# Attention with a memory, then a gated feed-forward: all pacing waits taken out, the order of issue written anew

## The chip, the cores and the metric

The kernel runs on one core of one Trainium2 chip. The metric is the device time of one execution in microseconds (us), the median of three runs. Engines are named as in the profile: PE (TensorE, matmul; PEld its weight loads), DVE (VectorE), ACT (ScalarE), POOL (GpSimd) and SP (SyncE, which here only issues DMAs).

## What is computed

Cut to what matters; all tensors are float32 at the kernel's border, and the three weight matrices come as float64.

```python
B, H, S, D = 4, 8, 576, 64
scores = causal(q @ k.T / sqrt(D));  a = softmax(scores)
local = a @ v
q_p = where(q > 0, q, exp(q) - 1) + 1
mem_out = (q_p @ M_prev) / (q_p @ z_prev + 1e-6)
g = sigmoid(beta)
x = g * mem_out + (1 - g) * local          # to (B*S, H*D) = (2304, 512)
xn = x / sqrt(mean(x * x) + 1e-6) * rms_g
gate = xn @ w_gate;  val = xn @ w_val      # d_ff = 1536
out = (gate * sigmoid(gate) * val) @ w_out # (2304, 512)
```

## The kernel before

**Tiling.** The 2304 rows are 18 blocks of 128. Blocks 0 to 3 are the first 128 rows of each of the four batches (one key block each) and are computed in float32; the others work on pairs of float16 numbers (a high and a low part). Two blocks make a chunk of 256 rows for the feed-forward part, so there are nine chunks, and each runs over 12 column blocks F of the hidden width. Chunk 0 is in float32 too.

**The lead-in.** Until about 160 us the kernel loads and prepares what later stages use. The 24 weight tiles of w_gate and w_val (W0 to W23; eight for each third of the hidden width, four of the gate and four of the value) and the 12 of w_out arrive as float64. `f64_to_f32` makes float32 of a tile with two ACT ops (lines 1023 and 1027) and one DVE op (line 1033). Later `w_split` makes float16 pairs. The scales for these pairs come from Gram matrices, `gram` (line 293, matmuls called csum), of keys, values and weights; those of keys and values of batches 0 and 1 need all their blocks, so `all_stats` loads blocks ahead of their turn: kv_602 is block 4 (two loads, keys and values), kv_605 the tail block of batches 0 and 1, kv_818 block 5, and `load_pre` (line 998) brings those called pre.

**The first blocks.** For block 0 and 1: transposes (tp, line 548), scores (line 614), exponentials on ACT (line 680), probabilities times values (loc, line 831), memory (mem, line 804). POOL adds both parts (line 849). `x_norm` squares and sums on ACT (line 408) and makes the factor xs on POOL (lines 908 and 911): x0 is that of block 0, x1 of block 1. `x_float` makes a diagonal of it on DVE (line 922), multiplies on PE (xtp, line 925) and writes xT on DVE (line 926). Then the first projections `m_proj` (gv, line 1110 in float32, line 1117 in float16) can run, and behind them the transposes of block 2.

**What sets the order.** A table, ISSUE, holds for each of the five engines the whole sequence of its instructions as a text: a letter is a kind of step, a number a repetition, and ~n takes the n-th of those not yet issued. `issue_in_order` chains all instructions of an engine in this sequence. Each engine works through its queue in that order. SP's loads share eight completion semaphores with ACT's, so a load waits for the one eight places ahead of it.

**The pacing waits.** On top of the true dependencies, some instructions wait on an event that they do not need, by `after` and `paced`. Five kinds there are: the first csum matmul of each key or value block of batch 0 and 1 waits for x0 (batch 0) or x1 (batch 1) (GDE); the loads of blocks 4, 5, of the tail and those of `load_pre` wait for x1 (GDL); the two ACT ops of conversions 2 to 11 wait for the last sum of block 1, event e11 (CDP, CDE); the memset and the copies of the second batch pair's memory matrix on POOL wait for x1 (lines 776 and 789); and the load of w_out tile f waits for the begin of conversion 20 + f (PACE). These lines state them:

```python
GDE = ("x0", "x1")
GDL = ("x1", "x1")
PACE = 4
CDP = (2, 12)
CDE = "e11"
```

Of the kernel before, what the change touches and what calls it, by code (L numbers as in the profile page):

```python
# [31 lines left out]
GDE = ("x0", "x1")  # L32
GDL = ("x1", "x1")
# [13 lines left out]
XP = 4  # L47
XB = 0
HLB = 5
RING = 5  # L50
PACE = 4
EARLY = 8
HTAG = ("v16", "v16", "v16", "v16")
CDP = (2, 12)
CDE = "e11"
# [12 lines left out]
GP = -600  # L68
# [1478 lines left out]
```

## Time and profile before

| | us |
|---|---|
| median of 3 runs | 604.43 |
| lowest and highest run | 602.52, 607.53 |
| the profiled execution, its own time | 602.39 |
| its span, first to last instruction | 600.5 |
| PE busy in it | 579.4 (96%) |
| DVE busy | 427.4 (71%) |
| ACT busy | 395.6 (66%) |
| POOL busy | 130.5 (22%) |

Times in the rows below are counted from the begin of the span; 1.9 us of the execution lie outside it. A row of the timeline gives the start, the time until the last end of a merged group, the engine, the line, the operation, what is written and read, the count, and in brackets the idle time of the engine before it with what ended it.

### The profile page before, as it was taken

To read this page: it belongs to the slowest core of one execution; us is meant where nothing else is said; L and a number is where in the kernel's file an instruction comes from. 1 tells how busy PE (TensorE), PEld (TensorE's weight loads), DVE (VectorE), ACT (ScalarE), POOL (GpSimd) and SP (SyncE) were. 2 spreads that over 40 slices of the span, in tenths; PEclk is the share of its full clock that TensorE was granted. 3 is DMA by queue.
4 is the path that set the end of the run, shared out by engine and by line. 5 is a ranking of instruction groups with operands and counts; after the bars stand their busy time and mean duration, and the time that the engine had idled before them with its cause. 6 is when DMAs were issued, how large, how long until landed. Compare 5 with 4: busy or idle time off the path is not lost.

```text
span 600.5 us, 15733 instructions
## 1 busy us (share of the span) xinstructions
PE 579.4 (96%) x6082; PEld 454.3 (76%) x6082; DVE 427.4 (71%) x1278; ACT 395.6 (66%) x856; POOL 130.5 (22%) x219
## 2 busy tenths in 40 slices
PE   6899999999899999999999999999999998999996
PEld 5778887678677778777777777777878776777774
DVE  3777998999998767776866777987885666642221
ACT  5889697998887667576657677876774454533221
POOL 2310012033332222131202221222122212121211
PEclk9899999999999999999999999999999999999999
DMA  7999555678879877977495789578884375441001
GB/s 249 365 319 395 152 172 157 154 155 160 189 138 182 136 137 164 147 149 147 85 186 125 135 157 170 117 140 142 137 166 80 70 115 97 86 67 28 10 1 53
DMA packets 183788, 87.57 MB, mean 146 GB/s; under 512 B 165793, under 2 KB 165793, under 8 KB 183713
## 3 DMA queue, kind: packets, MB, share of 16 engines
q1 hardware_dynamic: 180640, 81.82, 63.8%
q10 hardware_dynamic: 3072, 4.74, 2.4%
q8 instruction: 48, 0.79, 0.6%
q14 instruction: 28, 0.22, 0.1%
HBM read 37.77 MB, written 4.72 MB: 71 GB/s over the span
## 4 chain that ended last, share of the span: by engine, by line
PE 69%; DMA 15%; DVE 7%; ACT 6%; issue 2%; SPq 1%; POOL 0%; ACTq 0%; DVEq 0%; POOLq 0%
PE gv L1117 31%; PE out L1191 6%; PE out L1192 6%; PE out L1193 6%; DMA PT<-P 5%; PE gv L1110 4%; PE sc L625 4%; PE csum L293 2%; DMA kv<-in_qkv_dram 2%; DMA wgv<-in_moe_w_val_dram 2%; ACT junk L408 1%; PE sc L648 1%; PE loc L763 1%; DMA wgv<-in_moe_w_gate_dram 1%; PE loc L745 1%
## 5 line engine op out<-in xcount | busy, mean ns | idle before, releaser
L1117 PE MATMUL gv<-xT,wgv 128*128 128x256 f16 x2304 | 328.5, 273 | 2.0 <-DVE th L1138 2.0
L1117 PEld LDWEIGHTS <-wgv 128*128 128x128 f16 x2304 | 213.9, 98 | 47.2 <-issue 1.7
L1156 POOL TENSOR_TENSOR h<-th,h 128x256 f16<-128x256 f32 x88 | 64.8, 739 | 251.2 <-ACT h L1155 225.5
L688 ACT ACTIVATE S<-S,nm 128x256 f32<-128x256 f32 (+3 forms) x112 | 70.5, 639 | 39.9 <-DVE nm L631 19.7
L625 PE MATMUL sc<-kT,qT 128*128 128x128 f16 x576 | 85.2, 219 | 0.8 <-DVE nm L631 0.4
L1135 DVE SCALAR_TENSOR_TENSOR th<-th,gv 128x256 f32<-128x256 f32 x96 | 40.0, 416 | 63.0 <-ACT th L1134 61.6
L707 DVE SCALAR_TENSOR_TENSOR P<-S,P 128x512 f16<-128x512 f32 (+2 forms) x96 | 66.7, 695 | 24.1 <-ACT P L202 23.9
L1134 ACT ACTIVATE th<-gv,wt 128x256 f32<-128x256 f32 x96 | 44.9, 467 | 56.8 <-PE gv L1117 53.4
L202 ACT ACTIVATE P<-S 128x512 f16<-128x512 f32 (+2 forms) x96 | 57.8, 605 | 12.8 <-DMA PT<-P 11.7
L1191 PE MATMUL out<-wo,h 128*128 128x512 f16 x176 | 65.7, 379 | 0.2 <-ACT res L1168 0.2
L1192 PE MATMUL out<-wo,h 128*128 128x512 f16 x176 | 65.6, 379 | 0.0
L1193 PE MATMUL out<-wo,h 128*128 128x512 f16 x176 | 65.6, 379 | 0.1
L631 DVE CUSTOM_DVE_ANT_0 S<-sc,mask,qsc 128x256 f32<-128x256 f32 (+2 forms) x96 | 57.8, 610 | 10.6 <-PE sc L625 10.0
L1155 ACT CAST h<-th 128x256 f16<-128x256 f32 x88 | 34.8, 398 | 36.5 <-DVE th L1138 34.4
L625 PEld LDWEIGHTS <-qT 128*128 128x128 f16 x576 | 50.6, 98 | 9.9 <-issue 1.0
L745 PE MATMUL loc<-v,PT 128*128 128x65 f16 x288 | 46.0, 193 | 3.4 <-DMA PT<-P 2.4
L1138 DVE SCALAR_TENSOR_TENSOR th<-th,wt,gv 128x256 f32<-128x256 f32 x96 | 45.6, 476 | 1.3
L1110 PE MATMUL gv<-xT,wgv 128*128 128x256 f32 x192 | 46.5, 384 | 0.0
L747 PE MATMUL loc<-v,PT 128*128 128x65 f16 x288 | 46.2, 193 | 0.0
L746 PE MATMUL loc<-v,PT 128*128 128x64 f16 x288 | 45.3, 193 | 0.0
L1110 PEld LDWEIGHTS gv<-xT,wgv 128*128 128x128 f32 x192 | 34.9, 192 | 7.1 <-issue 1.9
L896 POOL TENSOR_TENSOR t<-t,t 128x256 f32<-128x256 f32 x28 | 21.3, 764 | 64.2 <-DVE t L893 60.1
(226 smaller groups left out, 980.0 us busy)
## 6 DMA issues: line engine op xcount, KB each, us to landing
kv<-in_qkv_dram SPq DMA_DIRECT2D x40, 256.0 KB, 3.8
q<-in_qkv_dram SPq DMA_DIRECT2D x18, 256.0 KB, 3.9
wo<-in_moe_w_out_dram SPq DMA_DIRECT2D x8, 512.0 KB, 4.6
out_dram<-res ACTq DMA_DIRECT2D x16, 256.0 KB, 2.4
wo<-in_moe_w_gate_dram SPq DMA_DIRECT2D x7, 512.0 KB, 7.9
wgv<-in_moe_w_val_dram SPq DMA_DIRECT2D x7, 512.0 KB, 8.7
qT<-qT SPq DMA_DIRECT2D x28, 128.0 KB, 3.0
wgv<-in_moe_w_gate_dram SPq DMA_DIRECT2D x5, 512.0 KB, 7.9
```

The costliest lines, as they stand in the source:

```text
L202: got = fn(*p, **k)
L625: nc.tensor.matmul(t[:, g * w + j * P : g * w + (j + 1) * P], qT[n][:, t2, h, :], kT[blk_of[(b, j)]][:, h, :], start=(t2 == 0), stop=(t2 = ...
L631: nc.vector.tensor_tensor_reduce(out=s[:, g * w : (g + 1) * w], in0=t[:, g * w : (g + 1) * w], in1=mask[:, m0 : m0 + w], scale=qsc[n][:, 5 ...
L688: nc.scalar.activation(v_, v_, AF.Exp, bias=nm[:, g : g + 1], scale=-1.0)
L707: m = nc.vector.scalar_tensor_tensor(out=p16[:, w : 2 * w], in0=s[:, :w], scalar=PSCALE, in1=p16[:, :w], op0=ALU.mult, op1=ALU.subtract)
L745: nc.tensor.matmul(a, phi_, vhi, start=(j == 0), stop=False)
L1110: nc.tensor.matmul(o, wgv[:, 1 + p, o0 : o0 + P], xT[0][:, cc, at], start=(cc == 0), stop=(cc == NC - 1))
L1117: nc.tensor.matmul(o, lhs, xT[c][:, rhs, :], start=(cnt == 0), stop=(cnt == 3 * NC - 1))
L1156: nc.gpsimd.tensor_tensor(h16[:, 1], th, h16[:, 0], ALU.subtract)
L1191: nc.tensor.matmul(o, hh, whi, start=(f == 0), stop=False)
L1192: nc.tensor.matmul(o, hh, wlo, start=False, stop=False)
L1193: nc.tensor.matmul(o, hl, whi, start=False, stop=(f == NF - 1))
```

## The change

All five kinds of pacing wait are taken out, with what served them (`after`, `paced`, the events, the priority around `gram`). No operation is added or removed and no buffer changes. The table ISSUE is written anew for all five engines; it holds the same instructions. The core of the diff, with a line or two of the table:

```diff
-GDE = ("x0", "x1")
-GDL = ("x1", "x1")
...
-PACE = 4
...
-CDP = (2, 12)
-CDE = "e11"
...
 ISSUE = {
     "PE": (
-        "T3T~1T~1T3Z2T12SS~1S~2S~3S3T4S2S~1S~2S~3T4uS4hu3h2ThT4u~2Tu2T2h4uT4h8ss~3ss~2ss~1s~1R3R~1R~1R~1R~1RsZG3G~5G~5G~5"
...
+        "T8Z2T12SS~1S~2SS~2S2T4uS2S~1S~2S~3T4S4uhu2h2sT2hT4u~2TuTuh4uT4h4s~3s~3h4s~3s~3ss~6sR3R~1R~1R~1R~1Rss~4s~4s~4G2G~"
...
-            m = nc.tensor.matmul(acc[:, :P], w, w, start=first and g == 0, stop=last and g == 3)
-            if g == 0 and ev:
-                after(m, event[ev])
+            nc.tensor.matmul(acc[:, :P], w, w, start=first and g == 0, stop=last and g == 3)
...
-            ins = nc.sync.dma_start(out=stage[n][:, j], in_=qkv[at_row[n], :, j, :])
-            if ev:
-                after(ins, event[ev])
+            nc.sync.dma_start(out=stage[n][:, j], in_=qkv[at_row[n], :, j, :])
...
-                with tc.high_priority(GP):
-                    gram(csum["kv", b, j], src[j][r], i == 0, i == NI, GDE[b])
+                gram(csum["kv", b, j], src[j][r], i == 0, i == NI)
...
-        m = nc.gpsimd.memset(mb, 0.0)
-        if pr:
-            after(m, event['x1'])
+        nc.gpsimd.memset(mb, 0.0)
...
-            m = nc.gpsimd.tensor_copy(pairs[b // 2][r, b % 2, :, t * D : t * D + D], m4[r, :, t, :])
-            if b > 1:
-                after(m, event['x1'])
+            nc.gpsimd.tensor_copy(pairs[b // 2][r, b % 2, :, t * D : t * D + D], m4[r, :, t, :])
...
-        if p - PACE in begun:
-            tc.add_manual_dep(
...
-            ins = nc.sync.dma_start(out=t, in_=qkv[at_row[blk_of[(b, i)]], :, j, :])
-            if GDL[b]:
-                after(ins, event[GDL[b]])
+            nc.sync.dma_start(out=t, in_=qkv[at_row[blk_of[(b, i)]], :, j, :])
...
-        begun[p] = nc.scalar.activation(dst, r[:, :, 1], AF.Prelu, scale=2.0 ** -112, alpha=2.0 ** 32)
-        late = CDP[0] <= p < CDP[1]
-        if late:
-            after(begun[p], event[CDE])
-        m = nc.scalar.activation(
+        nc.scalar.activation(dst, r[:, :, 1], AF.Prelu, scale=2.0 ** -112, alpha=2.0 ** 32)
+        nc.scalar.activation(
...
-        if late:
-            after(m, event[CDE])
```

What the table sets is shown at three places. The line numbers of the changed kernel are its own: 293 is again csum, 815 is loc, 908 xtp, 833 the sum on POOL, 891 and 894 the two ops of xs, 951 a weight load, 357 a kv load.

PE, before, at the end of the first two blocks' attention (loc_370 is that of block 1, kv_96 holds block 0, csum_608 and csum_613 gather keys and values):

```order
L548 MATMUL tp<-ident,S 128x128 x4
L831 MATMUL loc_370<-kv_101,PT_293 128x64 x4
L831 MATMUL loc_370<-kv_101,PT_341 128x64 x4
L293 LDWEIGHTS kv_96
L293 MATMUL csum_608<-kv_96 128x128
```

Six further csum follow there, and then xtp. PE of the change, at the same place:

```order
L543 MATMUL tp<-ident,S 128x128 x4
L815 MATMUL loc_370<-kv_101,PT_293 128x64 x4
L293 LDWEIGHTS kv_96
L293 MATMUL csum_613<-kv_96 128x128
L293 LDWEIGHTS kv_96
L293 MATMUL csum_613<-kv_96 128x128
L815 MATMUL loc_370<-kv_101,PT_341 128x64 x4
```

Two csum now stand between the loc matmuls; one more stands some rows ahead of these, five behind them, and then xtp. One of the five, and three between xtp and gv, read a half of kv_602, which before was read behind the first 32 gv only.

POOL, before, around the two factors xs (t_0 and t_1 are the sums of block 0 and 1):

```order
L849 TENSOR_TENSOR t_0_315<-t_0_315,t_0_338 128x4x64 x2
L908 TENSOR_SCALAR xs<-xs 128x1
L849 TENSOR_TENSOR t_1_328<-t_1_328,t_1_377 128x4x64 x2
L911 TENSOR_TENSOR xs<-xs,few 128x1
L908 TENSOR_SCALAR xs<-xs 128x1
L911 TENSOR_TENSOR xs<-xs,few 128x1
```

POOL of the change, the same instructions:

```order
L833 TENSOR_TENSOR t_0_315<-t_0_315,t_0_338 128x4x64 x2
L891 TENSOR_SCALAR xs<-xs 128x1
L894 TENSOR_TENSOR xs<-xs,few 128x1
L833 TENSOR_TENSOR t_1_328<-t_1_328,t_1_377 128x4x64 x2
L891 TENSOR_SCALAR xs<-xs 128x1
L894 TENSOR_TENSOR xs<-xs,few 128x1
```

The second op of x0 now stands ahead of block 1's two sums instead of behind them.

SP, before, from the second load of block 0 on (a gate tile that goes to wo is one of the second third, one that goes to wgv here is one of the first):

```order
L359 DMA kv_96<-in_qkv_dram 128x512
L985 DMA wo<-in_moe_w_gate_dram 128x512 x2
L985 DMA wgv<-in_moe_w_gate_dram 128x512
L372 DMA wo<-in_M_prev_dram 64x512
L985 DMA wgv<-in_moe_w_gate_dram 128x512
L403 DMA q_192<-in_qkv_dram 128x512
L985 DMA wgv<-in_moe_w_val_dram 128x512
L985 DMA wo<-in_moe_w_gate_dram 128x512
L985 DMA wgv<-in_moe_w_gate_dram 128x512
L387 DMA kv_2_0_194<-in_qkv_dram 128x512
```

SP of the change, from the same load on:

```order
L357 DMA kv_96<-in_qkv_dram 128x512
L368 DMA wo<-in_M_prev_dram 64x512
L399 DMA q_192<-in_qkv_dram 128x512
L357 DMA kv_101<-in_qkv_dram 128x512
L951 DMA wo<-in_moe_w_gate_dram 128x512
L383 DMA kv_2_0_194<-in_qkv_dram 128x512
L357 DMA kv_602<-in_qkv_dram 128x512
L951 DMA wgv<-in_moe_w_val_dram 128x512 x2
L951 DMA wgv<-in_moe_w_gate_dram 128x512
```

Two of the three gate tiles of the second third have moved behind the first eight tiles (one of them by 26 places, one by 11), and a half of kv_602 has come from place 30 of the queue to place 14. Further down, W15 moves from place 39 to 46, and the last halves of the pre loads of batch 1 by 4 to 9 places back. Over the whole table an instruction of DVE, ACT, POOL or SP stands on average one to five places from where it stood, one of PE two to eleven out of 5857.

## Rows read from the trace of the kernel before

**Rows 1.** Busy us by stretch: length, PE, PEld, DVE, ACT, POOL (x instructions), PE clock, DMA share, GB/s

```profile
22.70:26.20 3.50, 1.10 (x8) 0.97 (x8) 1.68 (x7) 0.93 (x3) 2.16 (x4) 0.93 1.00 397
26.20:32.56 6.36, 5.98 (x27) 5.26 (x28) 3.69 (x9) 5.74 (x13) 1.76 (x4) 0.50 1.03 348
32.56:39.40 6.84, 6.84 (x35) 5.94 (x34) 4.46 (x9) 5.64 (x11) 1.31 (x5) 1.00 1.02 282
39.40:43.30 3.90, 2.76 (x29) 2.25 (x26) 3.73 (x15) 2.74 (x6) 0.79 (x2) 1.00 1.01 331
43.30:105.00 61.70, 61.70 (x439) 51.36 (x438) 51.57 (x194) 50.98 (x118) 6.03 (x14) 1.00 0.65 222
105.00:165.00 60.00, 58.01 (x504) 43.32 (x504) 59.42 (x164) 54.73 (x120) 16.89 (x21) 1.00 0.78 164
165.00:585.00 420.00, 415.51 (x4869) 323.47 (x4867) 286.27 (x802) 256.73 (x534) 93.78 (x150) 1.00 0.65 118
```

**Rows 2.** Who waited for whom, 0 to 60 us: total us, times, longest us

```profile
ACT junk L408 <- POOL t L849: 2.6, 1, 2.6
...
PE csum L293 <- POOL xs L911: 1.8, 1, 1.8
...
PE csum L293 <- DMA pre<-in_qkv_dram: 1.0, 1, 1.0
```

**Rows 3.** PE in order of time, 23 to 42 us

```profile
23.26 1.10 PE L831 MATMUL loc<-kv,PT 128*128 128x64 f32 x8 [0.57 <-DVE t L847]
26.21 0.93 PE L293 MATMUL csum<-kv 128*128 128x128 bf16 x7 [1.84 <-POOL xs L911]
26.94 4.08 PE L925 MATMUL xtp<-diag,t 128*128 128x128 f32 x16
...
32.03 7.39 PE L1110 MATMUL gv<-xT,wgv 128*128 128x256 f32 x32
...
41.28 0.23 PE L293 MATMUL csum<-pre 128*128 128x128 bf16 x1 [1.01 <-DMA pre<-in_qkv_dram]
41.38 0.63 PE L548 MATMUL tp<-ident,kv 128*128 128x128 f32 x4
```

**Rows 4.** What SP's queue waited for, 26 to 60 us

```profile
SPq L359 <- POOL stt L413: 0.3, 1, 0.3
```

**Rows 5.** DVE in order of time, 24 to 32 us

```profile
24.41 0.42 DVE L847 TENSOR_TENSOR t<-loc,den 128x256 f32<-128x256 f32 x1 [0.38 <-PE loc L831]
26.19 0.29 DVE L922 TENSOR_SCALAR diag<-ident,xs 128x128 f32<-128x128 f32 x1 [1.36 <-POOL xs L911]
27.34 1.07 DVE L922 TENSOR_SCALAR diag<-ident,xs 128x128 f32<-128x128 f32 x1 [0.86 <-POOL xs L911]
...
30.63 1.29 DVE L926 TENSOR_TENSOR xT<-xtp,few 128x512 f32<-128x512 f32 x2 [1.81 <-PE xtp L925]
```

**Rows 6.** POOL in order of time, 23 to 27 us

```profile
23.18 0.19 POOL L908 TENSOR_SCALAR xs<-xs 128x1 f32<-128x1 f32 x1 [0.84 <-ACT junk L408]
24.03 0.72 POOL L849 TENSOR_TENSOR t<-t,t 128x256 f32<-128x256 f32 x1 [0.66 <-DVE den L842]
...
25.59 0.57 POOL L911 TENSOR_TENSOR xs<-xs,few 128x1 f32<-128x1 f32 x1
```

**Rows 7.** DMA issues, 0 to 60 us: count, KB each, median us to landing

```profile
kv<-in_qkv_dram SPq DMA_DIRECT2D x14, 256.0 KB, 8.3
...
wgv<-in_moe_w_val_dram SPq DMA_DIRECT2D x7, 512.0 KB, 8.7
...
pre<-in_qkv_dram SPq DMA_DIRECT2D x8, 256.0 KB, 5.8
...
M<-in_M_prev_dram SPq DMA_DIRECT2D x4, 128.0 KB, 7.9
```

**Rows 8.** ACT in order of time, at two places

```profile
25.66 0.63 ACT L408 ACTIVATE junk<-t 128x512 bf16<-128x512 f32 x1 [2.57 <-POOL t L849]
...
55.29 0.68 ACT L1023 ACTIVATE wgv<-wgv 128x512 f32<-128x512 f32 x1
```

**Rows 9.** SP's queue in order of time, at 43 us

```profile
43.52 0.66 SPq L359 DMA_DIRECT2D kv<-in_qkv_dram  x1
```

**Rows 10.** The weight loads of line 985, 0 to 70 us

```profile
DMA to landing us min/median/max: 3.5/7.8/11.2
```

More of the change, by code (lines that the diff above doesn't have):

```diff
@@ new lines @@
+        "6G~6G~6GG~5G2G~3G6Zs2Zs2Ts2T3s~2s~2T4sT2s2T2S8sG5s~4G3u2G2sGu2G5T4s~3ss~2ss~1ss~4s~4s3s~1s~1sT4G6g5g~11Zg5T4g5g~"
+        "1g~1g~1g~1g~1g~1g~1g~1g~1g~1Zg~1g~1g~1g~1g~1GgGh3G2ZG2TGZG2sGss~2s~2hT2s2s~2s~2Tss~1ss~1s~1s~1s2s~4s2s~2ss~1ss~1"
+        "s~1s~1s~1Ts~5s~5s~5s~5sTsGT2G3gG4g4h3sgs2hg2s4g14ZgZg2SS~1S~2S~3g~7g~7g~7g~7g~7g~7g~7g~7g2g~5g~5g~5g~5g~5gg~4S4g"
+        "TuGg5G3TG3gGu~1u~1T2Z2g9ug5DgD~1h4Z2DTGT3G4DGDGDGh3GhG6D~1DG~1G~1G~1G3DG3D6G4DG2G~2GG~1G~1G~1DG~1G20D~1SGD~2DGS~"
+        "7G8S~7G3DS~7GS~7S~7S~7G2S4S~3S3G2G~6G3M~8M~8MM~7GM~7M~7MM~6M~6SMGM4G3MG6SGS6G2SG2DMG3S3G3S4G3SGD2G15SG19S7ZG4PG7"
@@ L147 @@
+        "3kFl~1blrl~1l~1rkrL2FlL2blrLr~1rkL3l~1lFlL2XrL2bXr~1rkbL2lFL2rL2lr~1LXrkL2rL2Flr~1L3lLbXkrLlLlLFL3rLbLm~1XrL2l2r"
+        "mkL2FL4rXLrblklrL2kFL3bLl2L2rkl2r2FXbrLXLr~1rLklLlm2L2FL4bL3XrL2r~1krkLbFrr~1rkL2XFL3bLrL2XrkLrL2FLrL2rkLXLrLFL1"
+        "1X2"
     ),
@@ L285, in total, with gram @@
         return t[:, :n]
-    def gram(acc, src, first, last, ev=""):
+    def gram(acc, src, first, last):
         hi = src.bitcast(BF16).rearrange("p (f w) -> p f w", w=2)[:, :, 1]
@@ L354, in load_kv @@
     @keep("l")
-    def load_kv(n, ev=""):
+    def load_kv(n):
         tag = "kvt" if is_tail[n] else "kv"
@@ L716, in attn_memory_moe_kernel @@
     accs = {}
-    def after(ins, ev):
-        tc.add_manual_dep(
-            ins.ins, ev.ins.name,
-            mybir.DependencyInfo(mybir.DependencyClass.Sync, mybir.DependencyReason.SCHED_ONLY),
-            reason="pace",
-        )
     @keep("P")
@@ L848, in evac32 @@
         part = t1s[n][:, four(n, g4), :]
-        event["e%d%d" % (n, g4)] = nc.gpsimd.tensor_tensor(part, part, t2, ALU.add)
+        nc.gpsimd.tensor_tensor(part, part, t2, ALU.add)
     @keep("M")
@@ L950, in attn_memory_moe_kernel @@
     NR = RING
-    begun = {}
-    def paced(ins, p):
-        if p in (2 * NC + XP, 2 * NC + XP + 1) and XB in xdone:
-            tc.add_manual_dep(
-                ins.ins, xdone[XB].ins.name,
-                mybir.DependencyInfo(mybir.DependencyClass.Sync, mybir.DependencyReason.SCHED_ONLY),
-                reason="pace",
-            )
-        if p - PACE in begun:
-            tc.add_manual_dep(
-                ins.ins, begun[p - PACE].ins.name,
-                mybir.DependencyInfo(mybir.DependencyClass.Sync, mybir.DependencyReason.SCHED_ONLY),
-                reason="pace",
-            )
     def hold(p, at):
@@ L1011, in load_wo @@
         raws["o", f] = r
-        ins = nc.sync.dma_start(out=r.bitcast(I64), in_=w_out[f * P : (f + 1) * P, :])
-        paced(ins, len(pcs) + f)
-    event = {}
+        nc.sync.dma_start(out=r.bitcast(I64), in_=w_out[f * P : (f + 1) * P, :])
     @keep("U")
@@ L1277, in all_stats @@
         stat_begin(b)
-        load_kv(NA + b, GDL[b])
+        load_kv(NA + b)
         if b == 0:
-            load_kv(tails[0], GDL[b])
+            load_kv(tails[0])
         for i in range(NI + 1):
```

140 lines of the change are left out of this document (68 added, 72 removed).

## Prediction

> **What bounds the kernel now.** I read the busy time by stretches first [rows 1]. TensorE (PE) is the engine to watch: from 43.3 us to 105 us it is busy in 61.7 of 61.7 us, and from 165 us to 585 us in 415.5 of 420. What can still be won lies ahead of 43 us, and a little between 105 and 165 us, where PE misses 2.0 us and VectorE (DVE) is busy for 59.4 of 60 us. All five kinds of pacing wait stand in the first 110 us, so I looked there for what they cost. [...]
>
> Then I asked who waits for whom in the first 60 us [rows 2]. Two PE waits there touch the change. The statistics matmuls (csum, line 293) waited 1.8 us, once, for xs of line 911: this is a pacing wait (x0) itself. And a csum waited 1.0 us for a load called pre. PE in order of time shows what stands around them [rows 3]: eight loc matmuls at 23.26, an idle 1.84 us, seven csum at 26.21, the sixteen records of the first normed block pair (xtp) at 26.94, the first projections (gv, 32 records, 7.39 us) at 32.03, and the csum on pre at 41.28, behind which block 2's transposes stand in the same queue.
>
> **The change part by part.** *The waits themselves.* Of all that are taken out, the trace shows an engine stopping at two: the csum wait of 1.84 us, and 0.3 us on SP's queue, where a kv load (line 359) waits behind GpSimd (POOL) line 413, the op after x1 [rows 4]. The paced conversions on ScalarE (ACT) and the paced copies on POOL show no wait of their own: ACT idles 2.57 us ahead of the second square sum (line 408), but for POOL's line 849, its true input [rows 2]. So the waits alone are worth at most 1.84 + 0.3 = 2.1 us, and less where an engine behind them had nothing to do anyway: xtp needs the diagonal of line 922, which ran at 26.19 for 0.29 us [rows 5], so without the csum wait xtp would have begun at about 26.5 instead of 26.94, 0.4 us.
>
> *Statistics ahead of the lull (PE order).* The new order puts csum matmuls of block 0 between the loc matmuls, from 20 us on. They cost the same and fill time in which PE idles. By count, the 3.50 us before 26.2 us then hold 1.10 us, eight csum (seven took 0.93 us at the low clock, about half at the high one), and the first six xtp records (below), about 2.5 us in all.
>
> *Block 0's norm ahead of block 1's sum (POOL order).* Now line 911 for x0 stands behind both sums of block 1: line 908 is done at 23.37, and line 911 runs at 25.59 [rows 6]. In the new order 911 follows 908 at once, so x0 is there near 23.9. The sum that it is put ahead of began at 24.03, so it is not delayed. The diagonal then runs on DVE near 24.8, after the last line 847, and xtp's first six records (block 0) are done before block 1's diagonal, which keeps its 27.34 [rows 5]. Ten records are left. Sixteen took 4.08 us [rows 3], so ten take 2.55 us at the low clock, and about half at the high one: from 27.7 to 30.2 or 29.0 instead of 31.02. xT (two DVE ops, 1.29 us) and gv follow 0.8 to 2.0 us earlier, so gv begins between 30.0 and 31.2.
>
> *The clock.* Ahead of the low stretch PE did 1.10 us of work in 3.50 us [rows 1]; in the new order it is busier there, about 2.5 us, so I take it that the clock holds. The bounds are a low stretch as now, and one that is later and covers gv. [...]
>
> *Loads (SP order).* All are 256 KB (kv, pre) or 512 KB (weights), M 128 KB [rows 7]. In the new order one half of kv_602 comes forward by 16 places, ahead of seven of the first eight weight tiles (W0 to W7), and two gate tiles of the second third go behind them. Up to the last of the eight I count 8.4 MB before and 7.6 MB now, at 0.35 to 0.40 MB per us [rows 1] 2.0 to 2.3 us sooner. The conversions on ACT are then less held up too: behind the second square sum, which keeps its 25.66 [rows 8], 12 ops of about 0.57 us each stand until the eight tiles are converted, where there were 15: 1.7 us sooner. So weights do not hold gv, which ends 6.8 us (7.39 less the slow start) after it begins: between 36.9 and 38.7, depending on the clock.
>
> *The next wait.* Behind gv the first matmul that needs a late load is no longer csum on pre (11.25 MB into the queue, waited for until 41.28) but csum on the other half of kv_602, 10.5 MB in. 0.75 MB at 0.28 to 0.33 MB per us [rows 1] is 2.3 to 2.7 us, so it lands at about 38.8. That is later than gv's end at either clock. PE waits there, and block 2's transposes follow at 39.4 instead of 41.4: 2.0 us sooner. This load sets the gain, not the clock.
>
> *From there on.* From 43.3 to 105 us PE has no idle time, so what it starts sooner it ends sooner. DVE must follow, since it is the bound between 105 and 165 us; it is busy for 51.6 of 61.7 us before that, so it has 10.1 us of cover. If that cover were gone the 2.0 us would be lost. Everything behind is the same work in nearly the same order: instructions stand a few places from where they stood. I book 0, with 2 us to either side, the size of PE's loss in 105 to 165 us.
>
> The sum: the profiled execution took 602.39 us; less 2.0 is 600.4. The median of the three runs is 2.0 above that execution (604.43), so I predict 602.4.
>
> **The rivals.** *The order alone did the pacing.* In-order queues hold their order without any wait, so nothing but noise changes: 604.4. For it speaks that only 2.1 us of pacing waits can be seen; against it, that the csum wait stood on the way to gv.
>
> *The clock falls later, over gv.* If the low stretch begins at 28 and lasts 6.4 us as now [rows 1], gv begins at 31.2 and is slow until 34.4; in those 3.2 us it does 1.6 us of work, so it ends near 39.6 instead of waiting from 38.0 for the load that lands at 38.8. The gain is 0.8 less, 1.2: 603.2. It decides only from the point where gv ends behind 38.8.
>
> *Slower: a weight tile comes late.* With the pacing gone, loads that nobody needs yet stand ahead of needed ones: the last value tile of the second third (W15) moves from 12.5 MB into the queue to 15.25 MB. At 15.0 MB stands kv_818 now, and it is issued at 43.52 [rows 9]; so W15 would be issued near 44 and, with the 8.7 us of its kind [rows 7], land at 52.7. ACT converts it at 55.29 now [rows 8], at 53.3 if all runs 2.0 us ahead: 0.6 us of slack. With the 11.2 us of the slowest weight load [rows 10] it lands at 55.2, 1.9 us late, and as ACT's queue is in order, the scores, copies and conversions behind it stop too and the gain is gone. From there each further us goes onto the end; with W13, W14 and the pre loads of the second pair, which stand by it, late by 3 us in all it is 607.4. Against it: most of these loads have slack of some us. [...]
>
> *DVE turns out as the bound.* If the new order leaves DVE idle for half of its 10.1 us of cover more before 105 us, the saturated stretch behind it starts late: +5 and no gain, 609.4. Nothing in the profile asks for it, but nothing there is hidden either.
>
> **How the numbers follow.** A gain of 1 to 4 us as summed 0.48; the order alone 0.22; the clock 0.09; the late tile 0.11; DVE, or a like loss behind 165 us, 0.10. The predicted time is that of the first. The range takes in the second to fourth and most of the fifth at the top, and at the bottom 2.0 us for the open term and 2 us for the spread of runs (602.5 to 607.5): 598.0 to 609.4. Over 1% (about 6 us, what a measurement of this kernel can tell from no change) faster needs both of these at once and a clock that holds: 0.08. Over 1% slower is the last case and a part of the late tile: 0.12. Within 1%: 0.80.
>
> **What would show it.** Right: no csum wait on xs; xtp in two parts, the first near 25 us; gv from about 30 to 31 us; PE waiting for kv_602 near 38 us; block 2's transposes near 39.4; PE full until 105. The load term is wrong if PE waits past 40 us for kv_602, the clock term if the granted clock is 0.50 behind 33 us, the last term if PE's idle time behind 105 us differs by more than 2 us, and the whole if ACT waits for a weight load between 50 and 60 us.

## The result and the profile after

Six runs of each kernel on the same chip gave a median of 603.47 us before (601.17 to 607.53) and 597.01 us after (596.68 to 599.18). The ratio is 0.9892, with a 95% interval of 0.9848 to 0.9935. The forecast was 602.4 us (598.0 to 609.4): the direction was right, the gain was three times what was forecast, and it fell outside the range.

The two profiled executions are no typical pair. That of before (602.39 us) lies 1.1 us below its median; that of after (599.18 us, span 597.2) is the slowest of its six. So they show 3.2 of the 6.5 us between the medians. More sets of runs came with the experiments, and one plain fact about them is needed for every number below: the 97 runs of the kernel before fall into two groups with nothing between, 58 from 599.4 to 604.6 us (median 601.7) and 39 from 606.3 to 611.6 us (median 608.2). Over all 97 the median is 602.6. The changed kernel's 18 runs lie from 593.2 to 599.9 us, median 596.7, with no gap.

The busy time by stretches of the profile after, as [rows 1] of before (length, then busy us of PE, its weight loads, DVE, ACT and POOL, the granted clock, the DMA share, GB/s):

```profile
22.70:26.20 3.50, 2.41 (x21) 1.96 (x19) 1.89 (x7) 3.13 (x8) 2.22 (x4) 1.00 1.02 315
26.20:32.56 6.36, 3.55 (x18) 2.99 (x19) 4.40 (x9) 6.36 (x14) 2.59 (x7) 0.76 1.03 309
32.56:39.40 6.84, 6.84 (x25) 5.67 (x24) 3.04 (x7) 3.54 (x7) 1.58 (x4) 0.73 0.97 307
39.40:43.30 3.90, 3.90 (x34) 3.42 (x32) 2.74 (x12) 2.98 (x7) 0.00 (x0) 1.00 1.03 370
43.30:105.00 61.70, 61.70 (x438) 51.34 (x437) 53.73 (x201) 52.30 (x120) 5.75 (x11) 1.00 0.63 220
105.00:165.00 60.00, 58.43 (x515) 43.44 (x514) 54.54 (x163) 53.60 (x119) 15.68 (x23) 1.00 0.80 160
165.00:585.00 420.00, 417.77 (x4890) 325.65 (x4888) 286.98 (x802) 259.59 (x536) 93.20 (x152) 1.00 0.65 119
```

PE in order of time after, as [rows 3] (start, us until the last end of the group, operation, count, and in brackets the idle time ahead of it and what ended it; for the wait of 2.48 us the row names a conversion on DVE's line 989, but what these matmuls read is block 1's diagonal, and it ended at 28.34 us):

```profile
23.25 1.10 PE L815 MATMUL loc<-kv,PT 128*128 128x64 f32 x8 [0.47 <-DVE t L831]
...
25.07 0.94 PE L908 MATMUL xtp<-diag,t 128*128 128x128 f32 x6 [0.42 <-DVE diag L905]
28.48 1.56 PE L908 MATMUL xtp<-diag,t 128*128 128x128 f32 x10 [2.48 <-DVE wgv L989]
...
31.00 9.78 PE L1066 MATMUL gv<-xT,wgv 128*128 128x256 f32 x32 [0.52 <-DVE cb L460]
...
41.34 0.28 PE L543 MATMUL tp<-ident,kv 128*128 128x128 f32 x1
```

The csum wait of 1.84 us is gone, xtp comes in two parts, gv begins 1.0 us sooner. But the granted clock, which was low ahead of gv in [rows 1], is now low over gv (0.76 and 0.73 of full in the second and third stretch), so gv takes 9.78 us instead of 7.39, and block 2's transposes stand at 41.34 us, where they stood at 41.38 in [rows 3]. **In this execution the lead gained nothing.** The gain is further back: PE's idle time from 105 to 585 us is 3.80 us (1.57 and 2.23) against 6.48 us (1.99 and 4.49) in [rows 1].

Who waited for whom on PE from 105 to 585 us (us in total, times, longest us). Before:

```profile
PE loc L745 <- DMA PT<-P: 2.4, 4, 1.6
PE gv L1117 <- DVE th L1138: 2.0, 2, 1.7
PE loc L745 <- DVE t L874: 0.9, 1, 0.9
```

After:

```profile
PE loc L733 <- DMA PT<-P: 1.9, 3, 1.6
```

The three longest waits of before in this stretch, PE in order of time:

```profile
159.25 0.27 PE L1117 MATMUL gv<-xT,wgv 128*128 128x256 f16 x1 [1.66 <-DVE th L1138]
...
474.19 0.19 PE L745 MATMUL loc<-v,PT 128*128 128x65 f16 x1 [0.85 <-DVE t L874]
...
502.64 0.20 PE L745 MATMUL loc<-v,PT 128*128 128x65 f16 x1 [1.62 <-DMA PT<-P]
```

None of the three is left after. A new wait of 1.57 us stands there at 146.36 us, for transposed probabilities.

### The profile page after: what moved, and what is told of

It reads as the page before. It is cut to its first block, busy times and chain, and to the rows that moved or that the text cites. A ratio compares the mean times of both kernels' runs of the same rounds, so it can differ in the third digit from the quotient of the medians.

```text
span 597.2 us, 15713 instructions
## 1 busy us (share of the span) xinstructions
PE 577.9 (97%) x6082; PEld 453.3 (76%) x6082; DVE 422.9 (71%) x1278; ACT 397.3 (67%) x856; POOL 127.6 (21%) x219
## 4 chain that ended last, share of the span: by engine, by line
PE 87%; DMA 8%; ACT 1%; SPq 1%; DVE 1%; issue 1%; POOL 0%; ACTq 0%; DVEq 0%; POOLq 0%
PE gv L1073 38%; PE gv L1066 8%; PE out L1149 7%; PE out L1147 7%; PE out L1148 7%; PE sc L620 5%; PE out L1139 3%; DMA PT<-P 3%; DMA wgv<-in_moe_w_val_dram 3%; PE csum L293 2%; PE sc L643 1%; PE loc L751 1%; PE loc L733 1%; PE loc L734 1%; PE loc L735 1%; PE mem L849 1%
## 5 line engine op out<-in xcount | busy, mean ns | idle before, releaser
L1073 PE MATMUL gv<-xT,wgv 128*128 128x256 f16 x2304 | 342.4, 273 | 0.0
L1073 PEld LDWEIGHTS <-wgv 128*128 128x128 f16 x2304 | 210.8, 98 | 50.6 <-issue 2.8
L1112 POOL TENSOR_TENSOR h<-th,h 128x256 f16<-128x256 f32 x88 | 62.9, 719 | 255.0 <-ACT h L1111 229.7
L620 PE MATMUL sc<-kT,qT 128*128 128x128 f16 x576 | 90.9, 219 | 0.0
L702 DVE SCALAR_TENSOR_TENSOR P<-S,P 128x512 f16<-128x512 f32 (+2 forms) x96 | 65.3, 683 | 18.8 <-ACT P L202 18.4
L733 PE MATMUL loc<-v,PT 128*128 128x65 f16 x288 | 49.4, 193 | 1.9 <-DMA PT<-P 1.9
L1066 PE MATMUL gv<-xT,wgv 128*128 128x256 f32 x192 | 49.6, 400 | 0.5 <-DVE cb L460 0.5
L735 PE MATMUL loc<-v,PT 128*128 128x65 f16 x288 | 49.8, 193 | 0.0
L734 PE MATMUL loc<-v,PT 128*128 128x64 f16 x288 | 48.9, 193 | 0.0
L1066 PEld LDWEIGHTS gv<-xT,wgv 128*128 128x128 f32 x192 | 36.2, 200 | 9.7 <-issue 4.0
```

The source lines that it names most:

```text
L620: nc.tensor.matmul(t[:, g * w + j * P : g * w + (j + 1) * P], qT[n][:, t2, h, :], kT[blk_of[(b, j)]][:, h, :], start=(t2 == 0), stop=(t2 = ...
L702: m = nc.vector.scalar_tensor_tensor(out=p16[:, w : 2 * w], in0=s[:, :w], scalar=PSCALE, in1=p16[:, :w], op0=ALU.mult, op1=ALU.subtract)
L735: nc.tensor.matmul(a, plo, vhi, start=False, stop=(j == nb - 1))
L1066: nc.tensor.matmul(o, wgv[:, 1 + p, o0 : o0 + P], xT[0][:, cc, at], start=(cc == 0), stop=(cc == NC - 1))
L1073: nc.tensor.matmul(o, lhs, xT[c][:, rhs, :], start=(cnt == 0), stop=(cnt == 3 * NC - 1))
L1112: nc.gpsimd.tensor_tensor(h16[:, 1], th, h16[:, 0], ALU.subtract)
```

## The experiments

The theories after the result: **A**, the gain comes from the order behind the lead (from about 105 us on), where PE's stalls went; **B**, it comes from the waits taken out and the lead's order, and the trace of after only hides it; **C**, a part of it is the upper group of the kernel before, which has a cause of its own. Orders of the two kernels are joined thus: what the kernel before began ahead of a given time stands first, in one kernel's order, on all engines; the rest follows in the other's. A diff of the table then shows only the first line that differs.

**The waits alone, and the two halves of the order.** e1 is the changed code with the old table:

```diff
 ISSUE = {
     "PE": (
-        "T8Z2T12SS~1S~2SS~2S2T4uS2S~1S~2S~3T4S4uhu2h2sT2hT4u~2TuTuh4uT4h4s~3s~3h4s~3s~3ss~6sR3R~1R~1R~1R~1Rss~4s~4s~4G2G~"
+        "T3T~1T~1T3Z2T12SS~1S~2S~3S3T4S2S~1S~2S~3T4uS4hu3h2ThT4u~2Tu2T2h4uT4h8ss~3ss~2ss~1s~1R3R~1R~1R~1R~1RsZG3G~5G~5G~5"
```

> The changed kernel's code, so without any pacing wait, with the order of issue of the kernel before on all five engines. Theory A (the gain comes from the rewritten order behind the lead, from about 105 us on): as before, ratio 0.998 to 1.003, about 603 us. Theory B (the gain comes from taking the waits out, in the first 110 us): ratio 0.988 to 0.992, about 597 to 598 us. My own sum put the waits alone at 2.1 us at most (ratio 0.9965).

e2 has the new lead (100 us) and the old order behind it:

```diff
-        "TuGg5G3TG3gGu~1u~1T2Z2g9ug5DgD~1h4Z2DTGT3G4DGDGDGh3GhG6D~1DG~1G~1G~1G3DG3D6G4DG2G~2GG~1G~1G~1DG~1G20D~1SGD~2DGS~"
+        "TuGg5G3TG3gGu~1u~1T2Z2g9ug5DgD~1h4Z2DTGT3G4DGDGDGh3GhG4DG3DG4DG4D9G6G~2GG~1G~1G~1G~1G20DD~1SS~7G10S~7G3DS~7GS~7S"
```

> No pacing waits; the new order on all engines for the instructions that the kernel before began in its first 100 us, and behind them the old order. Theory A (order behind the lead): ratio 0.998 to 1.003 (602 to 605 us), with the stalls of before near 470 and 497 us back. Theory B (waits and order of the lead): ratio 0.988 to 0.992, and no stalls there.

e3 is the kernel before, waits and all, for its first 120 us, and the new order behind:

```diff
-        "4gTg3G4uG4u3T3ZgZg15DD~1h4Z2DTGDT3D~1G5DG2Dh3GhG7DG4DG4D9G6G~2GG~1G~1G~1G~1G20DD~1SS~7G10S~7G3DS~7GS~7S~7S~7GS4G"
+        "4gTg3G4uG4u3T3ZgZg15DD~1h4Z2DTGDT3D~1G5DG2Dh3GhG7DG4DG4D9G6G~2GG~1G~1G~1G~1G20DSGD~1GS~7G8S~7G3DS~7GS~7S~7S~7G2S"
```

> The code of the kernel before with all its pacing waits and its old order for what it began in its first 120 us, and behind that the new order. Theory A (order behind the lead): ratio 0.988 to 0.992 (597 to 598 us), PE as full between 465 and 585 us as in the changed kernel. Theory B (waits and order of the lead): ratio 0.998 to 1.003.

Measured (12 runs each): e1 600.5 us, ratio 0.9958 (0.9918 to 0.9998); e2 599.7, 0.9948 (0.9918 to 0.9978); e3 597.6, 0.9933 (0.9897 to 0.9969). All lie between the two theories' numbers, and the runs say why: e1 has nine runs from 598.6 to 601.2 and three from 604.5 to 606.6; e3 has eight from 596.0 to 598.1 and four from 601.5 to 602.8; e2 has one group. With the old lead there are two groups; by the lower ones e1 stands at 600.1 and e3 at 597.0, against 601.7 of before. So e3, with every pacing wait in its place, already has 4.7 us: theory A in the main, but only after the two groups are told apart. e2's trace has the stalls behind DVE (1.7 us) and behind the transposed probabilities (1.5 us) back, as A has it, and its median lies 2.0 us under the lower group of before: that is what the lead brings.

**The two groups.** The profiled run of e3 (602.79 us) is one of its upper group, and its first 120 us are the kernel before. PE at the start, in that execution:

```profile
11.34 2.67 PE L621 MATMUL sc<-k,q 64*128 64x128 f32 x14
13.94 1.12 PE L555 MATMUL tp<-ident,ph 128*128 128x128 f32 x4
...
23.64 1.06 PE L555 MATMUL tp<-ident,S 128*128 128x128 f32 x4
...
27.89 0.60 PE L555 MATMUL tp<-ident,S 128*128 128x128 f32 x4
```

and in the profile of before, which is of the lower group:

```profile
11.30 1.85 PE L614 MATMUL sc<-k,q 64*128 64x128 f32 x14
13.07 0.66 PE L548 MATMUL tp<-ident,ph 128*128 128x128 f32 x4
```

Both begin these scores at 11.3 us. Ahead of them four transposes take 1.06 to 1.12 us in the kernel before: from the start of one such group to the next operation it is 0.88 us there (8.49 to 9.37) and 0.44 us later (21.18 to 21.62), hence half rate. Then the kernel before goes over to full rate (0.60 to 0.66 us for four), and e3 stays at half until after 25 us. Its last loc of block 1 begins at 29.97 us instead of 23.26. So with one lead the moments, near 12 us and past 25 us, lie more than 13 us apart from one execution to the other; what sets the moment is not shown.

To try that PE's first microseconds decide it, k5 gives the kernel before six matmuls of the identity ahead of the first transposes, in time in which PE waits for the first load:

```diff
         t = ps.tile([P, NC, P], F32, tag="gv", name="tp")
+        for r in range(0 if warmed else 6):
+            nc.tensor.matmul(t[:, r % NC, :], ident, ident, start=True, stop=True)
+        warmed.append(1)
         for cc in range(NC):
```

> The kernel before, unchanged but for six matmuls of the identity ahead of TensorE's first transposes, in time in which PE waits for the first kv load (until 4.99 us). The runs of the kernel before so far fall into two groups, 600 to 604 us (20 of 29) and 606 to 609 us, and a trace that fell in the upper group of another kernel with the same lead shows every matmul from 11.3 to 27 us at half its rate. Theory C (PE starts at the low rate, and in the upper group it is let go 15 us later, because of what PE did in its first microseconds): all runs in one group, at 600 to 602 us, the median 0.5 to 2 us under that of before (ratio 0.995 to 0.999). Rival (the two groups come from the loads or from the chip, not from what PE did): again about a third of the runs 6 us above the others, ratio 1.000.

Measured: 12 runs from 598.7 to 601.3 us, median 600.7, ratio 0.9968 (0.9943 to 0.9994); none in an upper group, where before has 39 of 97 (9 of 29 on this chip in the same set). Theory C holds in this: with r3, r4 and b1 below, 30 runs of the old lead with this start show no upper group. How the six matmuls do it is not shown. In k5's own trace four transposes still take 1.12 us at 10.31 us and 0.66 us only at 12.87 us, as in that of before; in those of r4 and b1 they take 0.60 to 0.66 us from 8.32 and 8.57 us on. And the upper group was seen in one trace only, that of e3.

**The same separation with a warmed start.** Now the waits and the two halves of the order can be told apart. r3 is e1 with the six matmuls, r4 is e3 with them; b1 has the old lead without waits and the new order behind, b2 is the changed kernel with the six matmuls. The edit is that of k5 in each.

> No pacing waits, the old order on all engines, with six matmuls of the identity ahead of TensorE's first transposes. With the waits it took 600.7 us. If the waits cost what their rows show (1.84 us and 0.3 us): 598.5 to 599.5 us. If they cost nothing to the end: 600.5 to 601.

> The code of the kernel before with its waits and its old order in the first 120 us, the new order behind, and the six matmuls of the identity at the start. If the order behind the lead makes most of the gain: one group of runs at 596 to 597 us, 4 to 5 us under the 600.7 of the same without the new rest, and at most 1 us over the changed kernel. If the waits and the lead make it: 600 us.

> No pacing waits, the old order for what the kernel before began in its first 120 us, the new order behind, and the six matmuls of the identity at the start. With the waits it took 595.2 us (594.9 to 596.6). If the waits are worth what they were with the old order behind: 594.7 us, 0.5 less. If their rows (2.1 us) count now that nothing behind stalls: 593 to 593.5.

> The changed kernel with the six matmuls of the identity at the start alone. If the warm-up takes the late starts away here as it did with the old lead: one group of runs, at 594 to 595.5 us, none above 598. If it does harm in the new lead, as the run with both fillers suggests: 597 to 599 us, spread over 5 us or more.

Measured:

| kernel, all with six matmuls at the start | waits | lead | behind | median (range) us | runs |
|---|---|---|---|---|---|
| k5 | in | old | old | 600.74 (598.7 to 601.3) | 12 |
| r3 | out | old | old | 600.25 (599.2 to 601.7) | 6 |
| r4 | in | old | new | 595.20 (594.9 to 596.6) | 6 |
| b1 | out | old | new | 595.64 (594.2 to 597.1) | 6 |
| b2 | out | new | new | 593.43 (592.7 to 595.0) | 6 |

The waits alone: -0.5 us with the old order behind, +0.4 with the new one, so nothing that can be measured. The order behind the lead: -5.5 us (k5 to r4) and -4.6 (r3 to b1). The order of the lead: -2.2 us (b1 to b2). The sets ran on three chips, and sets of one kernel (the changed one: 597.0, 595.8, 595.3) differ by up to 1.7 us, so each of these holds to 1 or 2 us. On one chip each ran r3 and r4 (-5.1 us for the order behind, with the waits put back at the same time) and b1 and b2. e1 without the warming said -1.6 for the waits. From k5 to b2 it is 7.3 us in all; the 5.9 us between the medians of all runs of the two kernels as they are (602.6 and 596.7) mix this with late starts, executions in which PE leaves its half rate late.

The traces give the same shares. Busy time, kernel k5:

```profile
105.00:165.00 60.00, 58.03 (x510) 43.56 (x509) 59.41 (x167) 54.76 (x121) 16.88 (x21) 1.00 0.77 166
165.00:465.00 300.00, 298.14 (x3519) 234.66 (x3518) 231.08 (x660) 208.32 (x440) 69.94 (x115) 1.00 0.75 142
465.00:585.00 120.00, 117.64 (x1357) 89.61 (x1355) 55.46 (x141) 48.09 (x95) 23.91 (x36) 1.00 0.33 58
```

and kernel r4, which differs from it in the order behind 120 us alone:

```profile
105.00:165.00 60.00, 59.69 (x540) 44.72 (x540) 56.81 (x170) 54.93 (x121) 15.79 (x22) 1.00 0.78 167
165.00:465.00 300.00, 298.69 (x3513) 234.73 (x3512) 231.38 (x661) 212.21 (x443) 70.45 (x116) 1.00 0.76 142
465.00:585.00 120.00, 120.00 (x1374) 91.95 (x1373) 54.69 (x139) 47.02 (x93) 22.70 (x36) 1.00 0.31 61
```

PE's idle time falls from 6.19 to 1.62 us, 4.6 us of the 5.5, by 1.7, 0.6 and 2.4 us in the three stretches; DVE, busy for 59.4 of 60 us before, is at 56.8. For the lead, block 2's transposes in b1:

```profile
41.34 0.63 PE L547 MATMUL tp<-ident,kv 128*128 128x128 f32 x4
```

and in b2:

```profile
39.16 0.28 PE L548 MATMUL tp<-ident,kv 128*128 128x128 f32 x1
```

They come 2.18 us sooner, and the median is 2.2 us lower: what the lead gains is kept to the end. On the waits the traces of the old lead agree with the medians. With the waits these transposes stand at 41.38 us (before), 40.98 (k5) and 40.96 (r4), without them at 40.15 (e1), 41.12 (r3) and 41.34 (b1): neither side is clearly ahead.

**Where behind the lead, and on which engine.** k7 has the old order on all engines behind the first 440 us; m1 has it there on PE alone, m2 on the other four alone; r2 has the old order between 100 and 300 us. The first line that differs, in k7 and m1:

```diff
-        "~1P2G2P3G2MG3PGP2SPGP3G8DG3SDD~1MD~1D~1SGPSGSGP5G2PDP3GPGPGPGPGPGPMG4PG2D~3PD~3SGDD~2DM3SG2SMSG2S2G2PDP4G9PG2D~3"
+        "~1P2G2P3G2MG3PGP2SPGP3G8DG3SDD~1MD~1D~1SGPSGSGP5G2PDP3GPGPGPGPGPGPGPG5D~3D~3PMSGSG2SDD~2DM4SG2S2G2M2PDP4G7PG4PGP"
```

in m2 (ACT's table):

```diff
-            "ov~2Hv~1Ev~1CDv~1AE~1EHvCDHNACqfECXrEHACEACHkHkAECHAFrAHEkHEE~1CECfNAqXEE~2FHECECAErAHE~1CHE2CAODOD~1CHNCAqXfkEH"
+            "ov~2Hv~1Ev~1CDv~1AE~1EHvCDHNACqfECXrEHACEACHkHkAECHAFrAHEkHEE~1CECfNAqXEE~2FHECECAErAHE~1CHE2CAODOD~1CHNCAqXHfAk"
```

and r2 begins to differ where e2 does.

> No pacing waits, the new order up to what the kernel before began in its first 440 us, the old order behind. Theory A1 (most of the gain behind the lead is the stalls of before near 470 and 497 us, which the new order removes): PE busy for 117.5 to 118.5 of 120 us from 465 to 585 us, median 599 us, 2 us over the changed kernel. Theory A2 (it is the stretch of 105 to 165 us, in which VectorE is saturated): as the changed kernel, 597 us, PE at 120 of 120 us.

> The changed kernel, but TensorE alone has its old order behind what the kernel before began in its first 440 us; the other four engines keep the new one. With all five engines old there the median went up by 2.6 us (598.4 against 595.8). Theory P (the new PE order keeps loc away from its transposed probabilities until they have landed): 598 to 599 us, PE idle by 1.5 to 2.5 us between 465 and 585 us, ahead of loc. Theory Q (the order of ScalarE, VectorE and of the transposing DMAs makes the probabilities sooner): 595.8 to 596.5 us, PE full.

> The changed kernel, with the old order behind the first 440 us on ScalarE, VectorE, GpSimd and the DMA queue of SyncE, and the new one on TensorE. Theory P (PE's order makes the gain): 595.8 to 596.5 us. Theory Q (the others' order does): 598 to 599 us, with idle time of PE ahead of loc. If both this and the run with the old PE order lose 2 us or more, the gain is in the match of the two.

> The changed kernel with the old order put back for what the kernel before began between 100 and 300 us. If the stalls near 148 and 159 us (0.3 and 1.7 us, in which PE waits for VectorE) are worth what they show: they come back, and the median is 1 to 2 us over the changed kernel, 597 to 598. If VectorE's relief there is worth nothing: as the changed kernel.

Measured: k7 598.4 us (596.3 to 604.3, ratio 0.9933), 2.6 over the changed kernel on the same chip (595.8; 1.7 over its 18 runs). Its trace has the stall of 502.64 us back, ahead of the same loc, at 497.39 us there:

```profile
PE loc L732 <- DMA PT<-P: 1.7, 1, 1.7
```

m1 598.2 and m2 598.2 us, both 2.4 over the changed kernel's set on that chip (1.5 over its 18 runs), with six runs each, which spread over 3 to 4 us. In m1 PE waits elsewhere:

```profile
PE out L1148 <- POOL h L1111: 0.9, 1, 0.9
PE out L1146 <- ACT h L1110: 0.9, 1, 0.9
```

This speaks for a gain that neither side holds alone: PE's order and that of the engines that feed it must match, and with either one old something is late again. With differences of 1.5 to 2.4 us it is not shown beyond the spread of the sets. In m2 the rows show 0.7 us of waits and 0.9 us of idle time only; the rest of its 2.4 us I cannot place. r2 took 597.5 us, 2.2 over the changed kernel on its chip (595.3; 0.8 over its 18 runs), which is within the spread of these sets, but in its trace the waits of before are back:

```profile
PE gv L1070 <- DVE th L1091: 2.0, 2, 1.7
```

**The clock over gv.** e4 gives the changed kernel seven matmuls of the identity in the 2.48 us in which PE waits for block 1's diagonal. It ran in two sets on two chips.

```diff
         t = ps.tile([P, NC, P], F32, tag="sc", name="xtp")
...
+        for r in range(7 if n else 0):
+            nc.tensor.matmul(t[:, r % NC, :], ident, ident, start=True, stop=True)
         for cc in range(NC):
```

> The changed kernel with seven further TensorE matmuls of the identity, written into the second xtp tile just ahead of its true ones, so that PE has work in the 2.5 us in which it waits for the second diagonal. If idle time ahead of gv is what lets the clock fall, the granted clock stays at 1.0 through gv, which then takes 6.8 us instead of 9.8 and ends near 38.0. Theory A2 (the lead is then bound by the weight load that ACT converts at 38.64): block 2's transposes begin near 40.6 instead of 41.34, 0.7 us sooner, and the end comes 0 to 1 us sooner than that of the changed kernel: ratio to before 0.987 to 0.990. Rival (the lead is bound by PE alone): transposes near 38.5, the end about 3 us sooner, ratio 0.983 to 0.985. If the clock is set by something else, gv stays at 9.8 us and the ratio at 0.989.

> The changed kernel with the seven matmuls of the identity ahead of the second half of xtp, again, on the chip of these runs. Its first runs gave 594.2 us, 592.6 to 597.9; with six more ahead of the first transposes it was 597.4, 595.3 to 601.5, on another chip. If keeping the clock up over gv is worth 2 us: 593.5 to 595. If the gain of the first runs was that chip's: 596 to 597.5, as the changed kernel or over it.

Measured: 594.21 us (592.6 to 597.9), ratio 0.9865 (0.9821 to 0.9909), and 594.23 us (593.1 to 596.5), 2.5 us under the changed kernel's 18 runs and 1.6 under its set on the second of these chips. In the second trace the granted clock is 1.00 throughout the lead:

```profile
29.30 7.17 PE L1068 MATMUL gv<-xT,wgv 128*128 128x256 f32 x32 [0.93 <-DVE cb L460]
...
38.07 0.29 PE L293 MATMUL csum<-kv 128*128 128x128 bf16 x2 [1.38 <-DMA kv<-in_qkv_dram]
38.96 0.49 PE L271 MATMUL allp<-ident,ssm 128*128 128x128 f32 x2 [0.60 <-ACT junk L404]
...
39.40 0.27 PE L543 MATMUL tp<-ident,kv 128*128 128x128 f32 x1
```

gv takes 7.17 us instead of 9.78, then PE waits for the second half of kv_602 until 38.07 us and for ACT's square sum of a weight tile, and block 2's transposes begin at 39.40 (39.11 in the trace of the first set). In that first trace the clock was not kept up: it reads 0.50 from about 24.4 to 27.3 us, while the seven matmuls run, and 1.00 again over gv, which takes the same 7.17 us; there PE waits for ACT alone (0.60 us). A trace without the seven matmuls in which PE is slow ahead of gv and not over it looks alike: in r2 the ten xtp at 26.25 us take 2.47 us instead of 1.56, gv takes 7.17 us, and block 2's transposes begin at 38.90 us. So the second trace shows the mechanism of A2: once the clock is up, a late load and ACT bound the lead, not PE; in the first only ACT's 0.60 us is left of it. The size was off: the transposes come 1.9 to 2.2 us ahead of the 41.34 of the profile after, not 0.7, and in the second trace PE also left its half rate sooner (four transposes take 0.66 us from 11.21 us on, in that of after from 12.83 on; gv begins at 29.30 us, not 31.00).

The changed kernel itself ran twice more, for its traces:

> The changed kernel again, on the chip of these runs, for a second trace of it: 596.5 to 597.5 us, no run above 600. In the first trace of it the low granted clock covers gv (29.5 to 36.3 us). If where the low stretch falls differs from one execution to the next, this one may show it ahead of gv, block 2's transposes near 39 us instead of 41.3 and a span of 594 to 595 us; if the order sets it, it shows 41.3 us again.

> The changed kernel again, on the chip of these runs: 595.8 to 597.0 us as in its two sets so far, and a low granted clock over gv as in both traces, or, if where it falls differs by chance, ahead of gv.

Measured: 595.84 us (594.0 to 598.1) and 595.32 us (593.2 to 599.9). In a2's trace the low clock again covers gv (9.87 us from 30.43 on), with the transposes at 40.86. The trace of a3 (599.89 us, its slowest run) shows a late start in the changed kernel too:

```profile
15.74 1.11 PE L543 MATMUL tp<-ident,S 128*128 128x128 f32 x4
...
24.87 0.60 PE L543 MATMUL tp<-ident,S 128*128 128x128 f32 x4
```

No run is above 600, as expected, but I took the new lead to be free of late starts, and it is not. It has them shorter or rarer, and b2, where the six matmuls stand at the start, is 3.3 us under the 18 runs. In e2, with the lead of the changed kernel, the low stretch lay ahead of gv (24.0 to 30.8 us), and the transposes stood at 38.89. So where the low stretch falls differs from one execution to the next.

**Two that did not do what was expected.** k6 has both sets of matmuls, six at the start and seven ahead of xtp's second half.

> The changed kernel with the seven matmuls ahead of the second half of xtp as before, and six of the identity ahead of the first transposes. The first by itself gave 594.2 us. If PE's early rate is on the path, another 0.5 to 1.5 us: 593 us, ratio 0.984. If the early stretch is bound by loads, ACT and DVE, as 594.2, ratio 0.9865, perhaps with less spread.

Measured: 597.4 us (595.3 to 601.5, 12 runs), ratio 0.9912 (0.9877 to 0.9947), worse than with either set alone (593.4 and 594.2). Its trace is of its fastest runs and shows nothing wrong. Why the two together lose is open.

e6 has five matmuls there, and on POOL two short operations ahead of the memset of Mpair:

```diff
 L894 TENSOR_TENSOR xs<-xs,few 128x1
-L764 MEMSET Mpair 128x1040
 L409 MEMSET stt_816 128x15
-L767 COPY Mpair<-zz 64x8
 L479 COPY M_1_492<-zhl 128x16
+L764 MEMSET Mpair 128x1040
+L767 COPY Mpair<-zz 64x8
 L767 COPY Mpair<-zz 64x8
```

> The changed kernel with five matmuls of the identity ahead of the second half of xtp, and on GpSimd the 0.97 us memset of Mpair put behind two short operations, so that it begins when VectorE's second diagonal is done. In both traces of the changed kernel this diagonal takes 1.0 us, where the first takes 0.28, and the memset runs beside it. If the memset holds it up, the diagonal takes 0.3 to 0.6 us and xtp's second half begins 0.4 to 0.7 us sooner; with the clock up over gv block 2's transposes begin at 38.5 to 39.5 us and the median is 593.5 to 594.5. If not, the diagonal stays at 1.0 us, and the median at 594 to 595.

Measured: 594.85 us (593.7 to 597.5). The diagonal still takes 1.17 us:

```profile
24.71 1.17 DVE L905 TENSOR_SCALAR diag<-ident,xs 128x128 f32<-128x128 f32 x1 [2.32 <-POOL xs L894]
```

but the memset, at 24.81 us, still ran beside it: the two operations put ahead were too short to move it. An order that keeps the two fully apart was not tried. This stays open.

## Why the prediction was wrong, step by step

1. *The waits themselves*: right, as far as the sets can tell. I allowed 2.1 us at most and 0.4 us on the path; taking them out changed the median by -0.5 and +0.4 us with a warmed start, and by -1.6 us without it (e1).
2. *Statistics ahead of the lull*: right. PE is busy for 2.41 us of the 3.50, forecast 2.5.
3. *Block 0's norm*: right up to the diagonal (24.74 us, forecast 24.8) and for the six early records of xtp (25.07). The other ten began at 28.48, forecast 27.7. I had given the second diagonal the 0.29 us of the first, although [rows 5] show 1.07 us for it. gv still began at 31.00, within 30.0 to 31.2.
4. *The clock*: it did hold ahead of gv, as assumed (1.00 in the first stretch; the low stretch of before is the 0.50 of the second in [rows 1]), and then fell over gv, from about 29.5 to 36.3 us, after the 2.48 us in which PE waits for the diagonal. That is the rival "the clock falls later", and in the profiled run it went further than I had worked out: gv ended near 40.8 us, not 39.6. One term was too small: at the full clock gv takes 7.17 us (e4), where I booked 6.8. That PE's work ahead of gv holds the clock was my estimate, and no run shows it: with the same seven matmuls it reads 0.50 from about 24.4 to 27.3 us in e4's first trace and 1.00 throughout the lead in its second.
5. *Loads*: right. The first eight tiles were converted by 35.0 us instead of 37.0 in the profile of before.
6. *The next wait*: right in kind and place, but hidden behind the slow gv in the first trace. With the clock up (e4, second trace) PE waits for the other half of kv_602 until 38.07 us, forecast 38.8, and block 2's transposes begin at 39.40, forecast 39.4. With a warmed start the lead gains 2.2 us, forecast 2.0; that these lie so close is in part luck, since in b2's trace gv takes 9.23 us and PE waits for no load there.
7. *From there on*: **this step failed**. PE was full from 43.3 to 105 us, as said. But for all that lies behind I booked 0, "the same work in nearly the same order: instructions stand a few places from where they stood". That stretch gave 4.6 to 5.5 us (r3 to b1, k5 to r4). By the sign that the prediction itself set, PE's idle time behind 105 us off by more than 2 us, the last term was wrong in the first trace already: 6.48 us became 3.80. [rows 1] had the price in them: PE idle for 1.99 us and 4.49 us behind 105 us. I read 415.5 of 420 as full, and wrote that what can be won lies ahead of 43 us, with a little more up to 165. Most of the idle time was a handful of single stalls, the longest of 0.9 to 1.7 us, each in front of one loc or gv matmul, and an order that moved instructions by a few places on average took them out; which moves did it was not tried. Had I asked for the waits behind 105 us as I did for those ahead of 60, three rows would have named 5.3 us.
8. *The level and the spread*: I took the three runs of before (602.5 to 607.5) as one spread of 2 us to either side. They are from two groups 6.5 us apart, which go, as far as e3's trace and the 30 runs with a warmed start tell, by when PE leaves its half rate. The median of three (604.43) was 1.8 us above that of 97.

Of the rivals, "the order alone did the pacing" was right on the waits and wrong on the time. "A weight tile comes late" did not happen: between 45 and 62 us ACT waits for gv alone (1.5 us). "DVE turns out as the bound" went the other way: from 105 to 165 us DVE is busy for 54.5 us instead of 59.4.

The fastest kernel seen is b2, the changed kernel with six matmuls of the identity at the start: 593.43 us, ratio to before 0.9821 (0.9761 to 0.9882). The runs of before in that ratio come from both groups; set against the lower group alone (601.7 us) it is 0.986.

## What to carry to other kernels

When a table of order is written anew, list the single stalls of the busiest engine over the whole run, not only where the change is aimed: a share of 98.9% still held 4.5 us, most of it in one-off stalls that another order removed with the same instructions, and the two half-old tails (m1, m2) suggest that the queues on both sides of a stall have to match. The waits, whose rows showed little, were worth little when they went; ask what else the same edit moved. Before comparing medians, look at the runs one by one: two groups can mean two mechanisms, and a trace of each should be read.

## What the runs showed of the hardware

- PE runs at half rate at first: in the traces of before, after, e4 (second set), k5, k6, a2, a3, r2 and b2 four transposes in a row take 1.06 to 1.12 us there, later 0.60 to 0.66. The moment at which PE goes over to full rate differs by many microseconds: after the same lead it lay near 12 us in one trace (before) and between 25 and 28 us in another (e3). The runs of e3 lie at 601.5 to 602.8 us in the upper group, to which that trace belongs, and at 596.0 to 598.1 us in the lower. The changed kernel shows the moment near 12 us in two traces (four transposes take 0.66 us at 12.83 us in that of after and at 12.26 us in a2), and past 22 us in a third (a3: 0.76 us at 22.27, 0.60 us at 24.87).
- The granted clock does not show this. In the execution that ran at half rate until past 25 us, it reads 1.00 from 12 to 24 us, while from 16 to 20 us PE got through 19 matmuls where the kernel before got through 37. The number of matmuls in one stretch shows it:

```profile
16.00:20.00 4.00, 4.00 (x19) 3.54 (x18) 2.87 (x21) 2.35 (x12) 0.40 (x1) 1.00 1.02 378
```

  That is e3; the kernel before in the same stretch:

```profile
16.00:20.00 4.00, 4.00 (x37) 3.84 (x36) 3.89 (x27) 4.00 (x21) 0.40 (x1) 1.00 1.01 391
```

- A DVE operation of 0.28 us took 1.01 us beside a POOL memset. In the profile after, DVE:

```profile
24.74 0.28 DVE L905 TENSOR_SCALAR diag<-ident,xs 128x128 f32<-128x128 f32 x1
27.33 1.01 DVE L905 TENSOR_SCALAR diag<-ident,xs 128x128 f32<-128x128 f32 x1 [2.32 <-POOL xs L894]
```

  and POOL:

```profile
27.25 0.97 POOL L764 MEMSET Mpair<- 128x1040 f32 x1
```

  In the traces of before and after this diagonal ends about 0.1 us after the memset (28.41 against 28.32 us, and 28.34 against 28.22). No run here kept the two apart, so the cause is not shown.
